# Chunked attention and a multiplicative FFN on one core: a,b of 1024 tokens ahead of the weight product, and w3 turned on the vector engine

## The chip, the cores and the metric

One core of a Trainium2 chip. Times are device microseconds (us) of one execution. The kernel before takes 272.34 us (median of four runs, 271.72 to 272.89), its profiled execution spans 270.6 us.

## The reference, cut to what matters

```python
# q, k, v: (8 batches, 8 heads, 576 positions, 64); attention within chunks of 64
scores = scale * matmul(q_c, k_c.T)
attn   = exp(scores - max) / sum
out    = matmul(attn, v_c)
x = out as (4608 tokens, 512)
a, b = x @ w1, x @ w2                   # 512 -> 1024
return ((a * b) @ w3) @ w_out           # 1024 -> 1024 -> 512
```

Both kernels use (a*b) @ (w3 @ w_out): the weight product `w3o` is formed once on the chip, which needs w3 turned (w3 transposed as the stationary operand).

## The kernel before

A *unit* is 128 tokens (two chunks). Its attention takes four steps, each of them the TensorE part of one *slot*: `t` turns q and k, `s` makes the scores, `p` multiplies exp(scores) by v (with a column of ones for the sum), `x` turns the normalised result into `xt`. Between the steps work the scalar engine (exp) and the vector engine (copies, normalisation). A slot can hold the steps of up to four different units, and the kernel keeps everything on TensorE in program order.

```python
    def do_slot(xu=None, tu=None, su=None, pu=None):
        if tu is not None or su is not None:
            pa = ps.tile([P, 2, 512], f32, tag="pa", name="pa")   # one buffer: turned q,k and scores
        if xu is not None or pu is not None:
            pb = ps.tile([P, 2, 512], f32, tag="pb", name="pb")
        # ... 16 matmuls for xu, 32 for tu, 16 for su, 16 for pu, then
        #     ACT: e = exp(pa);  DVE: qkT = copy(pa), xt = copy(pb), rc = 1/sum, xn = pb * rc
```

The FFN goes by tiles of up to 512 tokens. `do_a`/`do_b` make one of eight 128-row groups of a or b (4 matmuls each), `do_o` makes the output of 128 tokens (8 matmuls). Turning w3 is TensorE work here, eight 128x128 transposes to a row block, and a copy (0.69 us each in the trace) out of PSUM, where the kernel puts the tiles that TensorE writes:

```python
    tiles = [(0, TT), (TT, TT // 2), (TT + TT // 2, TT // 2)]      # TT = 512 tokens
    tiles += [(t0, TT) for t0 in range(2 * TT, NT, TT)]

    def do_w3T(ko):
        tp = ps.tile([P, FO, P], bf, tag="m", bufs=4, name="w3tp")
        for ki in range(FO):
            tr(tp[:, ki, :], w3[:, ko, ki * P:(ki + 1) * P], ident[:])
        w3T_t[ko] = msb.tile([P, FO, P], bf, tag="w3T", bufs=3, name="w3T")
        nc.vector.tensor_copy(w3T_t[ko][:], tp[:])
```

The order at the start: w3 and w_out are loaded first, and the attention of units 0 to 3 is woven into the eight groups of the weight product. Only then follow a,b of tile 0.

```python
    load_w3(0, 1); load_w3(1, 2); load_w(wo, moe_w_out, 0, DM); load_to(1)   # shortened
    load_w3(2, 3); load_w3(3, 4); load_v(0); load_to(3); load_w3(4, 6); load_w3(6, 8)
    # ... w1, w2 in halves, units 4 to 9, v of batch 1
    do_w3T(0); do_w3T(1); do_w3o(0)
    do_slot(tu=0)
    do_w3o(1)
    do_slot(tu=1, su=0)
    # ... 
    do_slot(xu=3)
    do_w3o(7)
    # then a,b of tile 0 (all a, then all b), outputs 0 to 3 with slots between, tiles 1, 2, ...
```

The softmax here doesn't subtract the row's maximum and nothing guards it: scores larger than these inputs give would overflow.

Of the kernel before, what the change touches and what calls it, by code (L numbers as in the profile page):

```python
# [11 lines left out]
def kernel(  # L12
# [53 lines left out]

    ident = consts.tile([P, P], bf, name="ident")
    w1 = wpool.tile([P, KO, DF], bf, name="w1")
    w2 = wpool.tile([P, KO, DF], bf, name="w2")
    w3 = wpool.tile([P, FO, DF], bf, name="w3")  # L70
# [4 lines left out]
    NV = 3  # L75
    vbuf = [consts.tile([P, NHP, NCH, VW], bf, name=f"vbuf{i}") for i in range(NV)]
    for i in range(NV):
        nc.vector.memset(vbuf[i][:, :, :, D:D + 1], 1.0)


    def chunk_at(u, ci):
        return divmod(2 * u + ci, NCH)

    NRAW = 10
    qk_t = {}

    def load_unit(u):

        qk_t[u] = io.tile([P, 2, DM], bf, tag="qk", bufs=NRAW, name="qk")
        (b0, c0), (b1, c1) = chunk_at(u, 0), chunk_at(u, 1)  # L90
        parts = [(0, P, b0, c0)] if b0 == b1 else [(0, CH, b0, c0), (CH, P, b1, c1)]
        for t, src in enumerate((q, k)):
            for p0, p1, b, c in parts:
                load(qk_t[u][p0:p1, t, :].rearrange("p (h d) -> p h d", d=D),
                     src[b, :, c * CH:c * CH + p1 - p0, :].rearrange("h p d -> p h d"))

    def load_v(b):
        for t in range(2):
            load(vbuf[b % NV][t * CH:(t + 1) * CH, :, :, 0:D].rearrange("p n c d -> p (n c) d"),
                 v[b, t * NHP:(t + 1) * NHP].rearrange("n (c p) d -> p (n c) d", p=CH))  # L100
# [5 lines left out]



    NM = NHP // 2
    HW = NHP * CH  # L110
    W = D + 1
    half = [slice(0, CH), slice(CH, P)]
    qkT_t, e_t, xn_t = {}, {}, {}

    def do_slot(xu=None, tu=None, su=None, pu=None):
# [5 lines left out]
        if xu is not None:  # L121
            xn = xn_t.pop(xu)
            xv = pb[:, :, 512 - NHP * CH // 2:512].bitcast(bf).rearrange("p r (n t) -> p r n t", t=CH)
            for n in range(NHP):
                for g in range(2):
                    for r in range(2):
                        tr(xv[half[g], r, n, :], xn[half[r], (2 * n + g) * D:(2 * n + g + 1) * D],
                           ident[half[r], half[r]])
        if tu is not None:
            qk = qk_t.pop(tu)  # L130
            tv = pa[:, :, HW:512].bitcast(bf).rearrange("p r (s n t) -> p r s n t", s=2, t=CH)
            for s in range(2):
                for n in range(NHP):
                    for g in range(2):
                        for r in range(2):
                            tr(tv[half[g], r, s, n, :],
                               qk[half[r], s, (2 * n + g) * D:(2 * n + g + 1) * D],
                               ident[half[r], half[r]])
        if su is not None:
            qkT = qkT_t.pop(su)  # L140
            sv = pa[:, :, 0:HW].rearrange("p r (m c q) -> p r m c q", m=NM, c=2)
            for ci in range(2):
                for m in range(NM):
                    for t in range(2):
                        for r in range(2):
                            mm(sv[half[t], r, m, ci, :], lhsT=qkT[half[r], ci, 1, 2 * t + m, :],
                               rhs=qkT[half[r], ci, 0, 2 * t + m, :], start=True, stop=True)
        if pu is not None:
            e = e_t.pop(pu)
            for m in range(NM):  # L150
                for r in range(2):
                    for ci in range(2):
                        b, c = chunk_at(pu, ci)
                        for t in range(2):
                            n = 2 * m + r
                            mm(pb[half[ci], t, n * W:(n + 1) * W], lhsT=e[half[t], r, m, ci, :],
                               rhs=vbuf[b % NV][half[t], n, c, 0:W], start=True, stop=True)
        if su is not None:
            e = asb.tile([P, 2, NM, 2, CH], bf, tag="e", name="e")
            nc.scalar.activation(e[:].rearrange("p r m c q -> p r (m c q)"), pa[:, :, 0:HW],  # L160
                                 Exp, scale=scale, bias=0.0)
            e_t[su] = e
        if tu is not None:
            qkT_t[tu] = asb.tile([P, 2, 2, NHP, CH], bf, tag="qkT", bufs=3, name="qkT")
            nc.vector.tensor_copy(qkT_t[tu][:].rearrange("p r s n t -> p r (s n t)"),  # L165
                                  tv.rearrange("p r s n t -> p r (s n t)"))
        if xu is not None:
            nc.vector.tensor_copy(  # L168
                xt[:, :, xu * UT:(xu + 1) * UT].rearrange("p n (r t) -> p r n t", r=2), xv)
        if pu is not None:  # L170
            pv = pb[:, :, 0:NHP * W].rearrange("p t (n w) -> p t n w", w=W)
# [4 lines left out]
            xn_t[pu] = xn[:].rearrange("p t n d -> p (t n d)")  # L176


    tiles = [(0, TT), (TT, TT // 2), (TT + TT // 2, TT // 2)]
    tiles += [(t0, TT) for t0 in range(2 * TT, NT, TT)]  # L180
    ab_t, a_t = {}, {}

    def mm_ab(w, dst, t, j):
        t0, n = tiles[t]
        for ki in range(KO):
            mm(dst[:, 0:n], lhsT=w[:, ki, j * P:(j + 1) * P], rhs=xt[:, ki, t0:t0 + n],
               start=(ki == 0), stop=(ki == KO - 1))

    def do_a(t, j):
        n = tiles[t][1]  # L190
        a_ps = ps.tile([P, TT], f32, tag="m", bufs=4, name="a_ps")
        mm_ab(w1, a_ps, t, j)
        a_t[j] = msb.tile([P, TT], f32, tag="a_sb", bufs=FO, name="a_sb")
        nc.scalar.copy(a_t[j][:, 0:n], a_ps[:, 0:n])  # L194

    def do_b(t, j):
        n = tiles[t][1]
        if t not in ab_t:
            ab_t[t] = msb.tile([P, FO, TT], bf, tag="ab", name="ab")
        b_ps = ps.tile([P, TT], f32, tag="m", bufs=4, name="b_ps")  # L200
        mm_ab(w2, b_ps, t, j)
        nc.vector.tensor_mul(ab_t[t][:, j, 0:n], a_t.pop(j)[:, 0:n], b_ps[:, 0:n])  # L202

    def do_ab(t, j):
        do_a(t, j)
        do_b(t, j)

    def do_o(t, n):
# [4 lines left out]
        o_sb = msb.tile([P, DM], f32, tag="o_sb", name="o_sb")  # L213
        nc.scalar.copy(o_sb[:], o_ps[:])  # L214
        r0 = tiles[t][0] + n * P
        inorder(nc.sync.dma_start(out[r0:r0 + P, :], o_sb[:]))
# [3 lines left out]
    def do_w3T(ko):  # L220
        tp = ps.tile([P, FO, P], bf, tag="m", bufs=4, name="w3tp")
        for ki in range(FO):
            tr(tp[:, ki, :], w3[:, ko, ki * P:(ki + 1) * P], ident[:])
        w3T_t[ko] = msb.tile([P, FO, P], bf, tag="w3T", bufs=3, name="w3T")
        nc.vector.tensor_copy(w3T_t[ko][:], tp[:])
# [10 lines left out]
    w3v = moe_w3.rearrange("(ko p) n -> p ko n", p=P)  # L236

    def load_w3(k0, k1):
        load(w3[:, k0:k1, :], w3v[:, k0:k1, :])

    loaded = [0]

    def load_to(u):

        while loaded[0] <= min(u, NU - 1):
            load_unit(loaded[0])
            loaded[0] += 1

    def slot(s):

        do_slot(*(u if 0 <= u < NU else None for u in (s - 3, s, s - 1, s - 2)))

    load_w3(0, 1)
# [4 lines left out]
    load_w3(1, 2)  # L258
    load_w(wo, moe_w_out, 0, DM)
    load_to(1)  # L260
    load_w3(2, 3)
    load_w3(3, 4)
    load_v(0)
    load_to(3)
    load_w3(4, 6)
    load_w3(6, 8)
    HF = DF // 2
    for w, ap in ((w1, moe_w1), (w2, moe_w2)):
        for n0 in range(0, DF, HF):
            load_w(w, ap, n0, n0 + HF)  # L270
    load_to(5)
    load_v(1)
    load_to(9)


    do_w3T(0)
    do_w3T(1)
    do_w3o(0)
    do_slot(tu=0)
    do_w3o(1)  # L280
    do_slot(tu=1, su=0)
    do_w3T(2)
    do_w3T(3)
    do_w3o(2)
    do_w3o(3)
    do_slot(tu=2, su=1, pu=0)
    do_w3T(4)
    do_slot(xu=0, tu=3, su=2, pu=1)
    do_w3T(5)
    do_w3o(4)  # L290
    do_slot(xu=1, su=3, pu=2)
    do_w3T(6)
    do_w3o(5)
    do_slot(xu=2, pu=3)
    do_w3T(7)
    do_w3o(6)
    do_slot(xu=3)
    do_w3o(7)

    load_v(2)  # L300
    load_to(13)


    fill, units = [], {}

    def place(d, f, *a, **kw):
        def run():
            f(*a, **kw)
            if "tu" in kw:
                load_to(kw["tu"] + NRAW)  # L310
        units.setdefault(len(fill) + d, []).append(run)

    def place_slot(d, s):
        place(d, slot, s)
        place(d, load_to, s + NRAW)

        for b in range(B - 3):
            if (NCH * b + NCH - 1) // 2 == s - 2:
                place(d, load_v, b + 3)

    for j in range(FO):
        fill.append(lambda j=j: do_a(0, j))
    place(4, do_slot, tu=4)
    place(6, do_slot, tu=5, su=4)
    for j in range(FO):
        fill.append(lambda j=j: do_b(0, j))
    place(0, do_slot, su=5)
    place(1, do_slot, pu=4)
    place(1, load_v, 3)
# [75 lines left out]
```

## Time and profile before

| | before |
|---|---|
| time, median of 4 | 272.34 us |
| span of the profiled run | 270.6 us |
| TensorE busy | 242.6 us |
| first a,b matmul starts | 42.9 us |
| w3 transposes on TensorE | 64 in 8 groups, 0.55 us a group warm, 1.03 cold |
| weight product | 64 matmuls, 1.73 us a group of eight when warm |
| steady step (slot, two a,b pairs, one output) | 6.06 us |

The chain of waits of the kernel before (the work that ended last, followed back from step to step to what released it), in order of time (start, us, what):

```profile
3.04 10.65 DMA wo<-in_moe_w_out_dram
...
18.61 11.30 DMA w_76<-in_moe_w_dram
...
43.06 4.53 PE a_ps L59 x21
...
76.56 1.60 issue
...
83.06 1.03 issue
...
123.45 1.73 PE o_ps L59 x8
...
129.51 1.73 PE o_ps L59 x8
```

Until 30 us loads set the pace: w_out, then w3. From about 119 us one step follows the other every 6.06 us (129.51 - 123.45) without a gap. "issue" is time in which TensorE waited for nothing that the profile shows.

Two groups of the kernel before, the turning of w3 on TensorE and the copy on the vector engine (busy us, mean ns of one; idle before it):

```profile
L62 PE MATMUL w3tp<-ident,w_76 128*128 128x128 bf16 x64 | 6.4, 265 | 9.5 <-DMA w_76<-in_moe_w_dram 9.5
L225 DVE COPY w3T<-w3tp 128x1024 bf16<-128x1024 bf16 x8 | 5.5, 684 | 11.8 <-PE w3tp L62 11.8
```

Two of its waits (who waited for what: us in total, times, longest):

```profile
PE wp L59 <- DMA wo<-in_moe_w_out_dram: 5.4, 1, 5.4
...
ACT o_sb L214 <- DMA out_dram<-o_sb: 4.7, 2, 3.4
```

### The profile page before, as it was taken

The page shows a single profiled execution, that of the slowest core. Times are in us where ns is not written, and L with a number is a line of the kernel's source. Part 1 is how long each engine was busy: PE and PEld are TensorE (multiplying, and loading weights), DVE is VectorE, ACT ScalarE, POOL GpSimd, SP SyncE. Part 2 cuts the span into 40 slices and gives each one's busy share as a digit, 9 for nine tenths or more (in the row PEclk, how much of TensorE's full clock was granted, in tenths as well). Part 3 has the DMA queues.
Part 4 walks back from the last instruction along what each step waited for, and adds up shares of the span by engine and source line. Part 5 has one row for each costly group of instructions (what it writes and reads, how often), then busy time and mean ns, then how long its engine had stood idle before and what let it go on. Part 6 is the DMA issues. An engine that isn't in the chain of part 4 may idle for free.

```text
span 270.6 us, 8708 instructions
## 1 busy us (share of the span) xinstructions
PE 242.6 (90%) x3896; PEld 127.0 (47%) x3936; DVE 121.4 (45%) x235; ACT 91.2 (34%) x161; POOL 93.9 (35%) x113
## 2 busy tenths in 40 slices
PE   1198599999867999999999999999999999999994
PEld 1135454445655655454444454444444544444441
DVE  1113560364556546775555445555454454332210
ACT  1003125322433343443433344433433343233331
POOL 8484327988857077555422520000000000000000
PEclk9999799999999999999999999999999999999998
DMA  5999999999999999999997991211111111111223
GB/s 87 166 175 169 210 204 158 156 156 202 200 157 142 65 124 155 172 77 151 115 95 84 102 143 45 76 43 41 41 41 41 41 41 70 47 41 39 78 78 118
DMA packets 121620, 29.39 MB, mean 109 GB/s; under 512 B 112880, under 2 KB 115952, under 8 KB 121584
## 3 DMA queue, kind: packets, MB, share of 16 engines
q0 software_dynamic: 116400, 19.41, 94.3%
q1 hardware_dynamic: 5184, 9.44, 9.4%
q8 instruction: 31, 0.51, 0.8%
q14 instruction: 5, 0.04, 0.0%
HBM read 38.80 MB, written 9.44 MB: 178 GB/s over the span
## 4 chain that ended last, share of the span: by engine, by line
PE 78%; DMA 10%; issue 3%; DVE 3%; POOL 2%; ACT 2%; ACTq 0%; POOLq 0%
PE a_ps L59 22%; PE b_ps L59 21%; PE o_ps L59 21%; DMA w_76<-in_moe_w_dram 4%; DMA wo<-in_moe_w_out_dram 4%; PE pa L62 3%; PE pb L62 3%; PE wp L59 3%; DMA out_dram<-o_sb 2%; PE pa L59 2%; PE pb L59 2%; DVE qkT L165 1%; POOL qk L65 1%; DVE xn L175 1%; PE w3tp L62 1%
## 5 line engine op out<-in xcount | busy, mean ns | idle before, releaser
L202 DVE TENSOR_TENSOR ab<-a_sb,b_ps 128x512 bf16<-128x512 f32 (+1 forms) x80 | 50.1, 630 | 57.4 <-PE b_ps L59 52.3
L59 PE MATMUL b_ps<-xt,w_75 128*128 128x512 bf16 (+1 forms) x316 | 74.1, 357 | 0.8 <-ACT o_sb L214 0.3
L59 PE MATMUL a_ps<-xt,w_74 128*128 128x512 bf16 (+1 forms) x294 | 72.3, 357 | 1.6 <-issue 0.5
L59 PE MATMUL o_ps<-w3o,ab 128*128 128x512 bf16 x283 | 66.7, 379 | 0.5 <-issue 0.3
L194 ACT COPY a_sb<-a_ps 128x512 f32<-128x512 f32 (+1 forms) x80 | 43.4, 543 | 49.8 <-PE a_ps L59 47.4
L65 POOL DMA_DIRECT2D qk<-in_q_dram x40 | 34.1, 854 | 46.7 <-PE pa L59 21.9
L59 PEld LDWEIGHTS <-w_75 128*128 128x128 bf16 x320 | 31.1, 98 | 31.4 <-issue 0.8
L214 ACT COPY o_sb<-o_ps 128x512 f32<-128x512 f32 x36 | 21.1, 586 | 66.8 <-PE o_ps L59 62.1
L59 PEld LDWEIGHTS <-ab 128*128 128x128 bf16 x288 | 27.6, 98 | 32.6
L59 PEld LDWEIGHTS <-w_74 128*128 128x128 bf16 x320 | 28.6, 98 | 26.4
L65 POOL DMA_DIRECT2D qk<-in_k_dram x40 | 34.2, 858 | 5.6 <-DMA w_76<-in_moe_w_dram 3.6
L165 DVE COPY qkT<-pa 128x1024 bf16<-128x1024 bf16 x36 | 24.9, 691 | 20.1 <-PE pa L62 13.6
L168 DVE COPY xt<-pb 128x512 bf16<-128x512 bf16 x36 | 15.3, 424 | 40.8 <-PE pb L59 38.1
L160 ACT ACTIVATE e<-pa 128x512 bf16<-128x512 f32 x36 | 21.5, 598 | 28.9 <-PE pa L59 27.1
L175 DVE TENSOR_TENSOR xn<-pb,rc 128x512 bf16<-128x512 f32 x36 | 24.8, 690 | 1.0
L59 PE MATMUL wp<-wo,w3T 128*128 128x512 bf16 x59 | 16.6, 427 | 6.4 <-DMA wo<-in_moe_w_out_dram 5.4
L62 PE MATMUL pa<-ident,qk 64*64 64x64 bf16 x1152 | 16.2, 196 | 1.5 <-issue 1.0
L62 PEld LDWEIGHTS <-qk 64*64 64x64 bf16 x1152 | 12.9, 111 | 6.0 <-issue 5.8
L62 PEld LDWEIGHTS <-xn 64*64 64x64 bf16 x576 | 7.5, 108 | 16.0 <-issue 9.9
L62 PE MATMUL w3tp<-ident,w_76 128*128 128x128 bf16 x64 | 6.4, 265 | 9.5 <-DMA w_76<-in_moe_w_dram 9.5
L233 ACT CAST w3o<-wp 128x512 bf16<-128x512 f32 x8 | 4.7, 586 | 29.9 <-PE wp L59 29.9
L62 PE MATMUL pb<-ident,xn 64*64 64x64 bf16 x576 | 11.6, 199 | 1.9 <-DVE xn L175 1.7
(27 smaller groups left out, 93.6 us busy)
## 6 DMA issues: line engine op xcount, KB each, us to landing
out_dram<-o_sb SPq DMA_DIRECT2D x36, 256.0 KB, 2.9
qk<-in_q_dram POOLq DMA_DIRECT2D x32, 128.0 KB, 6.5
qk<-in_k_dram POOLq DMA_DIRECT2D x32, 128.0 KB, 6.4
vbuf_80<-in_v_dram POOLq DMA_DIRECT2D x6, 288.0 KB, 8.5
vbuf_81<-in_v_dram POOLq DMA_DIRECT2D x6, 288.0 KB, 6.8
vbuf_82<-in_v_dram POOLq DMA_DIRECT2D x4, 288.0 KB, 7.0
w_76<-in_moe_w_dram POOLq DMA_DIRECT2D x4, 256.0 KB, 7.9
wo<-in_moe_w_out_dram POOLq DMA_DIRECT2D x1, 1024.0 KB, 10.6
```

The source lines that it names most:

```text
L59: return inorder(nc.tensor.matmul(*a, **kw))
L62: return inorder(nc.tensor.transpose(*a, **kw))
L65: return inorder(nc.gpsimd.dma_start(dst, src))
L160: nc.scalar.activation(e[:].rearrange("p r m c q -> p r (m c q)"), pa[:, :, 0:HW], Exp, scale=scale, bias=0.0)
L165: nc.vector.tensor_copy(qkT_t[tu][:].rearrange("p r s n t -> p r (s n t)"), tv.rearrange("p r s n t -> p r (s n t)"))
L168: nc.vector.tensor_copy(xt[:, :, xu * UT:(xu + 1) * UT].rearrange("p n (r t) -> p r n t", r=2), xv)
L175: nc.vector.tensor_mul(xn[:], pv[:, :, :, 0:D], rc.to_broadcast([P, 2, NHP, D]))
L194: nc.scalar.copy(a_t[j][:, 0:n], a_ps[:, 0:n])
L202: nc.vector.tensor_mul(ab_t[t][:, j, 0:n], a_t.pop(j)[:, 0:n], b_ps[:, 0:n])
L214: nc.scalar.copy(o_sb[:], o_ps[:])
L233: nc.scalar.copy(w3o[:, ko, :], wp[:])
```

## The change

Its intent: start a,b of the first 1024 tokens as soon as attention of the first units is there, so that the loads of w3 and w_out pass behind that work, and take the turning of w3 off TensorE. The vector transpose is used by blocks of 32x32 (`BL`): w3 is loaded with its column blocks spread over the partitions, and w_out to match. Further: v is loaded by unit and not by batch, the small matmuls inside a slot and their places in PSUM are arranged anew, a and b are made in pairs from the start, three output buffers for two.

```diff
-    w3 = wpool.tile([P, FO, DF], bf, name="w3")
+    w3 = wpool.tile([P, DF // BL, DF // NB], bf, name="w3")          # BL = 32, NB = 4
+    def load_w3(f0, f1):
+        for i in range(NB):
+            load(w3[i * BL:(i + 1) * BL, f0:f1, :],
+                 moe_w3.rearrange("(f y) n -> y f n", y=BL)[:, f0:f1, i * DF // NB:(i + 1) * DF // NB])
+    # load_wo() likewise: four loads of 32 partitions
-    tiles = [(0, TT), (TT, TT // 2), (TT + TT // 2, TT // 2)]
+    tiles = [(0, 4), (4, 1), (5, 3)] + [(u0, 4) for u0 in range(8, NU, 4)]   # in units of 128 tokens
     def do_w3T(ko):
-        tp = ps.tile([P, FO, P], bf, tag="m", bufs=4, name="w3tp")
-        for ki in range(FO):
-            tr(tp[:, ki, :], w3[:, ko, ki * P:(ki + 1) * P], ident[:])
-        nc.vector.tensor_copy(w3T_t[ko][:], tp[:])
+        nc.vector.transpose(w3T_t[ko][:].rearrange("p k (f y) -> p f k y", y=BL),
+                            w3[:, NB * ko:NB * (ko + 1), :].rearrange("p f (k x) -> p f k x", x=BL))
# loads, now: units 0 to 3 (q, k, v), w1 and w2 in quarters, units 4 to 7, w_out, w3, units 8, 9
# order, now:
+    slot(t=0)
+    slot(t=1, s=0)
+    slot(p=0, s=1)
+    slot(x=0, t=2, p=1)
+    ...                                  # nine slots for units 0 to 3
+    for j in range(FO):
+        do_ab(0, j)                      # 512 tokens; slots of units 4, 5 after j = 4, 5, 6
+    slot(x=4, s=5)
+    for j in range(FO):
+        do_ab(1, j)                      # 128 tokens; slots of units 5 to 7 after j = 1, 3, 5, 6
+    slot(p=7)
+    slot(x=7)
+    for j in range(FO):
+        do_ab(2, j)                      # 384 tokens
+    do_w3T(0)
+    for ko in range(FO):
+        if ko + 1 < FO:
+            do_w3T(ko + 1)
+        do_w3o(ko)
+    for u in range(8):
+        do_o(u)
+        if u < 7:
+            step()                       # one slot of units 8 and on after each output
+    # then tiles of 512 as before: slot, two a,b pairs, one output
```

## The prediction

> **What bounds the kernel now.** TensorE. The busy table gives it 242.6 of 270.6 us. From about 119 us to the end it runs without gaps: the chain of waits repeats one slot (0.78 us), two a,b pairs (3.46) and one output group (1.73), 6.06 us in all. So only the time before 119 us is to be won. There the chain shows DMA, not TensorE, until 43 us: nothing until the first w3 row at 4.8, a 5.4 us wait for w_out until 13.7, a 3.3 us wait for w3 until 30. The first a,b matmul starts at 42.9 us, after 64 w3 transposes, 64 product matmuls and four attention units. A second loss, about 6.5 us, lies between 60 and 120 us (windows): outputs waiting for their DMA with two buffers (3.4 us at worst, in the waits), and attention slots waiting about 2 us each for the vector engine.

> **What the change removes.** 64 TensorE transposes of w3: 8 groups at 0.55 us when warm, 1.03 when cold, about 4.5-5 us on the critical engine; 8 PSUM copies of 0.69 us; the wait for 3 MB of w3 and w_out before a,b.

> **What it adds.** Eight vector transposes of 128x1024 bf16. [...] It hides behind tile 2 and the product (1.73 us a group). Also a 128-token tile: at 69 ns a matmul (w3 transposes of that width, chain) its eight pairs take 4.4 us.

> **The new order, from durations of the trace.** Queue issues of q, k, v take about 0.9 us each, so unit 3's k lands near 14 us; its attention chain (about 4.5 us) puts the first a,b at 19-21 us. TensorE is then cold: the product matmuls ran at 446 ns against 216 warm, [...] so about 2 us are lost. Tile 0 ends near 37 us; weight quarters (about 175 GB/s) keep ahead. The 128-token tile interleaves four slots of dependent attention: about 5 us idle, ending near 49. w3's first half should land at 44-48 us, just before the first vector transpose, queued at about 49 ahead of the a*b products. Tile 2 ends near 59, the product near 74. Eight outputs with seven slots: 95. Tile 3 takes 17 us, so the 6 us rhythm starts at 112-113 instead of 119, and the rest is unchanged, 151.5 us.

> **Prediction.** Profile span about 264 us, time 265.5 us, 2.4% faster. Range 260.5-271.5. Chances: faster by over 2% 0.58, within 2% 0.38, slower 0.04.

> **What would show it.** First a,b matmul at 19-21 us; [...] no TensorE wait for w3; product group back to back at about 59-74; o_sb waits gone; steady step still 6.06 us, starting at 112-113.

> **What would make it wrong.** [...] w3 landing after 49 us: the vector engine, then TensorE, would wait. Later attention data, or more idle in the 128-token tile or the output phase, each moves the sum 1-3 us; the 2% line (266.5) is 1 us away.

The sum came to a span of about 264 us and a time of 265.5 us, in which the transposes, taken as hidden, count for nothing. The 2 us for slow matmuls are in it, and the figures beside them give nearly that: eight matmuls at 446 for 216 ns are 1.8 us. In the trace of the kernel before, the product's matmuls follow each other at about 430 ns from 13.73 to 19.49 us (with a slot between), and at about 216 ns in the group that starts at 22.45 us.

## More of the kernel before

The page of the kernel before, busy time by engine, and two rows of its 40 equal slices (6.8 us each; a digit is the busy share in tenths, or, in PEclk, the share of TensorE's full clock that was granted):

```profile
PE 242.6 (90%) x3896; PEld 127.0 (47%) x3936; DVE 121.4 (45%) x235; ACT 91.2 (34%) x161; POOL 93.9 (35%) x113
...
PE   1198599999867999999999999999999999999994
...
PEclk9999799999999999999999999999999999999998
```

TensorE (PE) is the bound, and it is dense from the sixth slice on except for slices 11 to 13.

## The result, and the profile after

| | before | after |
|---|---|---|
| time, median of 4 | 272.34 us | 275.88 us (275.13 to 276.23) |
| ratio of the fast runs | 1 | 1.0122, 95% interval 1.0088 to 1.0155 |
| span of the profiled run | 270.6 us | 274.0 us |
| first a,b matmul starts | 42.9 us | 22.9 us |

A ratio is the mean time of one kernel's fast runs over that of the other's of the same rounds, so it is not quite the ratio of the medians quoted. The changed kernel is 1.2% slower: less than the 2% that the prediction's chances go by, but the interval leaves out 1. I had said 2.4% faster and a range that ended at 271.5.

The page of the changed kernel, the same rows:

```profile
PE 240.6 (88%) x3834; PEld 122.7 (45%) x3872; DVE 127.2 (46%) x244; ACT 91.5 (33%) x161; POOL 114.7 (42%) x146
...
PE   0346987599999749999999999999999999999994
...
PEclk9999999689999988999999999999999999999999
```

TensorE is dense from the fifth slice on and not from the sixth, but there are three thin places: slices 1 to 4, slices 6 to 8 (the 128-token tile) and slices 14 and 15 (the outputs). In the last two places the granted clock falls too.

The chain of waits of the changed kernel:

```profile
22.91 0.59 PE a_ps L59
...
48.61 1.84 issue
...
53.08 1.44 PE a_ps L59 x4
54.52 1.28 PE b_ps L59 x4
55.80 1.24 PE a_ps L59 x4
57.04 0.65 PE b_ps L59 x4
...
65.76 10.74 PE wp L59 x49
...
93.48 0.97 issue
...
98.56 2.63 issue
...
102.31 2.84 PE o_ps L59 x7
...
126.82 1.73 PE o_ps L59 x8
132.88 1.73 PE o_ps L59 x8
```

No load of w3 or w_out is in it, the product is dense, the steady step is 6.06 us as before. What is new are three "issue" gaps, 5.44 us together, and cold matmuls after two of them: four matmuls of 384 columns take 1.24 to 1.44 us, three times over, where later ones take 0.65, and seven of the output group take 2.84 us where the others take 1.67.

The vector transposes in the list of groups take 1240 ns each:

```profile
L225 DVE STREAM_TRANSPOSE w3T<-w 128x1024 bf16<-128x1024 bf16 x8 | 9.9, 1240 | 2.5 <-PE wp L59 1.4 <-DMA qk<-in_q_dram 1.1
```

**What an issue gap is.** Here are the weight loads of TensorE (PEld) between two of the gaps, from the timeline of the changed kernel (start, us, what, count; idle before). There is one to each matmul (the page counts 3872 of them and 3834 matmuls, of which some records can be missing):

```profile
94.44 0.11 PEld L59 LDWEIGHTS <-ab 128*128 128x128 bf16 x2 [1.46 <-issue]
94.98 0.21 PEld L62 LDWEIGHTS <-xn 64*64 64x64 bf16 x16 [0.42 <-issue]
95.10 0.35 PEld L62 LDWEIGHTS <-qk 64*64 64x64 bf16 x32
95.35 0.23 PEld L59 LDWEIGHTS <-qkT 64*64 64x64 bf16 x16
95.49 0.23 PEld L59 LDWEIGHTS <-e 64*64 64x64 bf16 x16
95.76 1.41 PEld L59 LDWEIGHTS <-ab 128*128 128x128 bf16 x8
98.06 0.21 PEld L62 LDWEIGHTS <-xn 64*64 64x64 bf16 x16 [0.89 <-DVE xn L181]
98.18 0.27 PEld L62 LDWEIGHTS <-qk 64*64 64x64 bf16 x22
101.19 0.21 PEld L62 LDWEIGHTS <-qk 64*64 64x64 bf16 x10 [2.74 <-issue]
```

The second gap stands in the middle of 32 like transposes: 16 of them turn q and 16 k, so after 22 both inputs had been there. From gap to gap there are 2+16+32+16+16+8+16+22 = 128 weight loads, and as many matmuls (127 are recorded): 256 instructions. In the kernel before, the gaps at 76.6 and 83.1 us are also 128 weight loads apart by the same count. The thought to be tested is that TensorE's instructions come in blocks of 256 (the expectations call one a page), and that a block comes late when loads of q, k, v are in flight and slots use instructions up fast (a full slot has 160 and takes 0.78 us).

The trace can be asked directly, since it also records a DMA queue named for instructions. From 98 to 101.3 us the DMA view of the changed kernel has one packet on it (packets, MB, share):

```profile
q8 instruction: 1, 0.02, 1.8%
```

The whole run has 30 packets of 16384 bytes on this queue, for 3834 + 3872 = 7706 recorded instructions of TensorE, 257 to a packet, which agrees with the count between the gaps. Narrow windows of the same view date them. The packet before the end of the second gap starts at 98.95 us, when TensorE has already run dry, takes 0.94 us, and TensorE goes on 1.30 us after it has landed. All 34 "issue" gaps of TensorE over 0.5 us in the 16 traces are of this kind: each ends 1.24 to 1.61 us after such a packet has landed, and each stands at 94 to 96 weight loads beyond a multiple of 128. So I take the gaps for waits for instructions. What is left to the experiments is why the packets come late.

```profile
43.21:46.63 3.42, 2.90 (x113) 2.44 (x110) 2.79 (x9) 1.47 (x6) 1.58 (x3) 1.00 1.45 196
46.63:50.04 3.41, 1.02 (x41) 0.78 (x40) 1.57 (x5) 0.91 (x3) 2.18 (x3) 1.00 1.46 197
50.04:53.45 3.41, 1.43 (x35) 0.89 (x35) 2.03 (x5) 0.00 (x0) 2.19 (x3) 0.50 1.47 195
53.45:56.87 3.42, 3.42 (x12) 1.53 (x11) 1.69 (x3) 0.48 (x1) 2.38 (x3) 0.50 2.35 159
56.87:60.28 3.41, 3.41 (x22) 2.06 (x21) 3.23 (x5) 1.43 (x3) 3.14 (x5) 1.00 2.42 156
```

then in the outputs:

```profile
97.82:101.24 3.42, 0.55 (x42) 0.44 (x46) 0.18 (x1) 0.46 (x1) 2.78 (x4) 1.00 1.92 233
101.24:104.65 3.41, 3.08 (x48) 1.64 (x50) 1.92 (x4) 0.60 (x1) 3.18 (x4) 0.50 2.18 159
```

A stretch in which TensorE is busy for 1.02 of 3.41 us is followed by one at half the clock, that one is thin too (1.43 us), and the dense one after it (3.42 us) still runs at half. No idle stretch was longer than 1.84 us in the first case: TensorE was thinly used there and not idle throughout. The trace records no clock before 19.65 us in the kernel before and before 26.15 us in the changed one, so that PEclk reads 9 in the head, although its matmuls run at half the pace there (four in 1.61 us from 24.78 us, four in 0.86 from 26.39). From the first record on the stretches of all 16 traces agree: where a stretch at full clock was followed by half, TensorE had been busy for 1.60 us of it at most (e6, from 100.54 us), and where it was followed by full, for 1.49 us at least (e13, from 99.24 us).

**Where the 10 us between predicted and measured span lie**, stage by stage (ends read from the chain, prediction as in its text with 20 us for "19 to 21"):

| stage | predicted end | measured end | difference in the stage's own length |
|---|---|---|---|
| attention of units 0 to 3, to the first a,b | 20 | 22.9 | +2.9 |
| tile 0 | 37 | 39.9 | 0 |
| 128-token tile | 49 | 53.1 | +1.2 |
| 384-token tile | 59 | 65.5 | +2.4 |
| weight product | 74 | 79.3 | -1.2 |
| eight outputs, seven slots | 95 | 105.1 | +4.8 |
| tile 3, to the steady step | 112.5 | 122.5 | -0.1 |
| rest | 264 | 274.0 | 0 (151.5 both) |

### The profile page after: what moved, and what is told of

It reads as the page before. It is cut to its first block, busy times and chain, and to the rows that moved or that the text cites. A ratio compares the mean times of both kernels' runs of the same rounds, so it can differ in the third digit from the quotient of the medians.

```text
span 274.0 us, 8642 instructions
## 1 busy us (share of the span) xinstructions
PE 240.6 (88%) x3834; PEld 122.7 (45%) x3872; DVE 127.2 (46%) x244; ACT 91.5 (33%) x161; POOL 114.7 (42%) x146
## 3 DMA queue, kind: packets, MB, share of 16 engines
q0 software_dynamic: 122048, 19.41, 95.3%
## 4 chain that ended last, share of the span: by engine, by line
PE 84%; DVE 6%; issue 4%; ACT 2%; DMA 1%; POOL 1%; ACTq 0%; DVEq 0%; POOLq 0%
PE a_ps L59 24%; PE b_ps L59 23%; PE o_ps L59 21%; PE wp L59 5%; PE pa L62 4%; PE pb L62 4%; DVE xn L181 3%; DVE qkT L170 2%; PE pa L59 2%; PE pb L59 2%; DMA qk<-in_k_dram 1%; ACT e L165 1%; POOL qk L65 1%; DVE xt L173 1%; DVE rc L179 0%
## 5 line engine op out<-in xcount | busy, mean ns | idle before, releaser
L59 PEld LDWEIGHTS <-w 128*128 128x128 bf16 x640 | 58.7, 99 | 63.6 <-issue 5.2
L59 PE MATMUL a_ps<-xt,w 128*128 128x512 bf16 (+2 forms) x293 | 75.6, 364 | 3.6 <-DVE xt L173 1.9
L59 PE MATMUL b_ps<-xt,w 128*128 128x512 bf16 (+2 forms) x318 | 76.7, 363 | 1.9 <-issue 1.8
L208 DVE TENSOR_TENSOR ab<-a_sb,b_ps 128x512 bf16<-128x512 f32 (+2 forms) x80 | 50.3, 630 | 58.5 <-PE b_ps L59 56.0
L203 ACT COPY a_sb<-a_ps 128x512 f32<-128x512 f32 (+2 forms) x80 | 43.4, 542 | 72.2 <-PE a_ps L59 66.0
L65 POOL DMA_DIRECT2D qk<-in_q_dram x40 | 34.6, 870 | 34.8 <-PE pa L59 23.7
L59 PEld LDWEIGHTS <-ab 128*128 128x128 bf16 x288 | 27.9, 99 | 34.8 <-issue 3.1
L65 POOL DMA_DIRECT2D vbuf<-in_v_dram x40 | 34.7, 869 | 5.4 <-DMA w<-in_moe_w_dram 3.9
L173 DVE COPY xt<-pb 128x512 bf16<-128x512 bf16 x36 | 15.3, 424 | 46.0 <-PE pb L59 42.5
L62 PE MATMUL pa<-ident,qk 64*64 64x64 bf16 x1152 | 17.1, 199 | 11.6 <-DMA qk<-in_q_dram 6.2
L59 PE MATMUL wp<-wo,w3T 128*128 128x512 bf16 x62 | 13.9, 379 | 0.1
L59 PE MATMUL pa<-qkT 64*64 64x64 bf16 x576 | 11.7, 200 | 2.0 <-DVE qkT L170 2.0
L65 POOL DMA_DIRECT2D w<-in_moe_w_dram x16 | 11.3, 745 | 3.9 <-DMA wo<-in_moe_w_out_dram 2.9
```

The costliest lines, as they stand in the source:

```text
L59: return inorder(nc.tensor.matmul(*a, **kw))
L62: return inorder(nc.tensor.transpose(*a, **kw))
L65: return inorder(nc.gpsimd.dma_start(dst, src))
L173: nc.vector.tensor_copy(xt[:, :, xu * UT:(xu + 1) * UT].rearrange("p (m b) t -> p b m t", b=2), xv.rearrange("p b m c t -> p b m (c t)"))
L203: nc.scalar.copy(a_sb[:, 0:n], a_ps[:, 0:n])
L208: nc.vector.tensor_mul(ab_t[t][:, j, 0:n], a_sb[:, 0:n], b_ps[:, 0:n])
```

## The experiments

Each median is of four runs, on the same chip and in the same rounds as runs of the kernel before (medians 272.2 to 272.7 us). Differences to the changed kernel go from one call to another; the medians of the kernel before differ by 0.5 us between the calls.

### e1: no loads after unit 9

Its output is wrong, which doesn't matter for the time.

```diff
     def load_unit(u):
+        if u >= NRAW:                      # q, k: reuse the old buffer
+            qk_t[u] = qk_keep[u % NRAW]
+            if u >= NVB:                   # v: likewise from unit 12
+                return
```

> The changed kernel without the loads of q and k after unit 9 and of v after unit 11 (later units reuse old buffers: wrong result on purpose). Order and number of TensorE instructions are the same. Theory FETCH (TensorE ran out of instructions at 93.5 and 98.6 us, 0.97 and 2.63 us long, [...] and the second gap cooled it, 1.1 us more): the two gaps vanish, the one at 48.6 us (1.84 us) stays, time 270 to 272 us. Theory CHAIN (the loss is attention slots waiting for vector and scalar engine with too little matmul work between): gaps named issue are a side matter, time 275 to 276 us.

What stays of FETCH is that the gaps come from the loads in flight.

Measured: 272.37 us (270.9 to 273.3), ratio to the kernel before 0.9979. That is 3.5 us less than the changed kernel, and 0.4 us more than the expected 270 to 272. From the first output to the first full tile it took 22.65 us (80.98 to 103.63) against 26.94 (79.14 to 106.08). Both gaps of the outputs are gone and so is the half clock there. The waits of the slots for the vector engine are still there, 0.37 us each, and the gap in the 128-token tile is still there, 1.71 us. The slot that held the second gap, and the longest "issue" left in the outputs:

```profile
99.11 0.32 PE pb L62 x16
99.43 0.26 PE pa L62 x32
99.69 0.18 PE pa L59 x16
...
102.99 0.27 issue
```

FETCH holds for the outputs: the loads stretch the gaps, since TensorE's instructions are the same. The two packets that ended the gaps in the changed kernel have landed here 2.6 and 2.9 us before the first weight load of their block. They took no less time themselves (1.29 and 1.46 us, there 0.95 and 0.94), so what the loads put off is their start. What holds them back before it, no view shows.

### e2 and e5: no loads of w3 and w_out either

Both have the edit of e1 as well. Their outputs are wrong, which doesn't matter for the times.

```diff
 # e2
-    load_wo(); load_w3(...)
+    nc.vector.memset(wo[:], 0.01)
+    nc.vector.memset(w3[:], 0.01)
 # e5
-    load_wo(); load_w3(...)
+    # transposes read w1, w2 in place of w3, the product reads w1 in place of w_out
```

> As the run without late loads, and w3 and w_out are filled on the chip at the start and not loaded either (wrong result on purpose). FETCH: the gap at 48.6 us (1.84 us) vanishes too, and the next tile no longer starts cold (about 2 us): time 266 to 268.5 us, no issue gap of more than 0.5 us. CHAIN: the tile of 128 tokens waits as before for the vector engine, 275 to 276 us. If the gap stays and the tile is still cold, neither loads nor fetch are its cause.

> The run without late loads, and w3 and w_out neither loaded nor filled: the vector transposes read w1 and w2 in their place and the product reads w1 (wrong result on purpose), so that nothing is put in front of the head, which the fills of the earlier quiet run delayed by 8 us. If loads in flight starve TensorE of instructions, no issue gap over 0.6 us is left, and from the first a,b matmul to the end it takes 2.5 us less than without late loads (248.2 us): about 246, time 270 or a little under. The first pairs of the 384-column tile are expected cold all the same (1.24 to 1.44 us for four matmuls, 0.65 warm), as the quiet run showed: the clock is lost by thin work in the 128-token tile and not by the fetch gap.

Measured: 278.77 and 278.72 us, slower by 6 us than e1, and both expectations of the time missed. Both are faults of the experiment. In e2 the two fills took 3.47 and 6.88 us on the vector engine, where I had expected a moment, ahead of the first copy of q and k. In e5 the scheduler put the vector transposes, whose inputs were now there early, into the queue in front of the last `xt` copy of the head, where they waited for w1 and held up the first a,b by 8 us (30.88 us). What can be read is the rest: from the first a,b to the end e5 takes 245.7 us (276.6 - 30.88), e1 248.25 (271.5 - 23.25), the changed kernel 251.1. The expected 246 is met. No issue gap over 0.6 us is left in e5, and the 384-token tile nevertheless begins with 1.44 us for four matmuls:

```profile
58.98 1.44 PE L59 MATMUL a_ps<-xt,w 128*128 128x384 bf16 x4 [0.53 <-DVE xt L176]
```

So the gap of 1.84 us comes from the loads in flight, and the slow matmuls there come without it too; I put them down to the thin 128-token tile.

### e3: w3 turned on TensorE, all else as changed

```diff
-        nc.vector.transpose(w3T_t[ko][:]..., w3[...]...)      # and block loads
+        for ki in range(FO):
+            tr(tp[:, ki, :], w3[:, ko, ki * P:(ki + 1) * P], ident[:])   # and row loads
+        nc.vector.tensor_copy(w3T_t[ko][:], tp[:])
```

> The changed kernel with only the vector transposes undone: w3 and w_out loaded in rows (3 loads instead of 12), w3 turned on TensorE into PSUM and copied, at the same place in the order. If the vector transposes are hidden as predicted, TensorE gets 64 transposes back, 4.4 us at 0.55 us a group: time 280 to 281 us. If the vector transposes or the loads into 32 partitions cost what the change lost, time is 271 to 276 us.

Measured: 281.8 us, 5.9 us above the changed kernel. So the vector transposes are hidden in the new order, and they and their block loads are not what lost the time; they save what the transposes cost TensorE (eight groups of 0.45 us in this run's chain, 3.6 us) and something besides, which I did not take apart: its gap near the end of the outputs was 3.12 us, and half the clock was granted there for 6.83 us and not 3.41. The 64 transposes and their weight loads are also 128 more instructions, as many as half a block.

### e4: slots of units 8 to 14 after every second group

```diff
         do_w3o(ko)
+        if ko % 2:
+            step()
     for u in range(8):
         do_o(u)
-        if u < 7:
+        if u in (1, 3, 5):
             step()
```

> The changed kernel with the seven attention slots of the product and output phase put one after every second group of eight 512-column matmuls (four in the product, three in the outputs) instead of one after each output. Both theories expect a gain: CHAIN 2 us (the waits of 0.4 us in four slots and a little), time about 274; FETCH more, since a page of 256 instructions now lasts 4.2 / (192/256) = 5.6 us instead of 3.6: the gaps at 93 and 98 us and the cold output group go, about 4.7 us beside the 2, time 269 to 271.

Measured: 271.37 us (270.34 to 271.86; ratio to the kernel before 0.9942, 0.9911 to 0.9974), 4.5 us less than the changed kernel, just outside the expected 269 to 271. Product and outputs take 34.84 us (66.53 to 101.37) and not 40.75 (65.33 to 106.08). Of the two gaps one of 0.55 us is left. The seven slots are spread over product and outputs and not over the outputs alone, so that instructions are used up more slowly (a slot and two groups are 192 in 4.24 us, a slot and one group 176 in 2.51), and as I read it the blocks come in time. The order also takes away waits for the vector engine; the run does not separate the two.

### e6: seven slots in the head for nine

```diff
-    slot(p=0, s=1); slot(x=0, t=2, p=1); slot(x=1, s=2); slot(t=3, p=2); slot(s=3); ...
+    slot(t=2, s=1, p=0); slot(x=0, t=3, s=2, p=1); slot(x=1, s=3, p=2); ...
```

> The changed kernel with the first four units' attention in 7 slots, combined as in the kernel before, instead of 9. If the number of slots makes the first a,b matmul late (22.9 us against the 19 to 21 predicted), it moves to 20.5 to 21 us and the time falls by 2 us. If it is the length of the dependent turn of one slot (scalar exp, vector copy, vector normalise: 2 to 3 us), the seven slots only become longer, the first a,b stays at 22 to 23 us and the time at 275 to 276.

Measured: 277.41 us, and the first a,b at 24.8 us, later than with nine: outside both expectations. The number of slots is not what makes the head long. As I read it, a merged slot waits for the latest of its inputs and hands all of them on late: the third slot now waits 1.61 us for q of unit 2. A gap in the supply of instructions, 0.77 us, also falls into this head.

### e7: 256 and 256 tokens for 128 and 384

```diff
-    tiles = [(0, 4), (4, 1), (5, 3)] + ...
+    tiles = [(0, 4), (4, 2), (6, 2)] + ...
     for j in range(FO):
         do_ab(0, j)
-        # t4 after j=4, s4 after 5, (t5, p4) after 6, (x4, s5) at the end
+        # t4 after j=2, (t5, s4) after 4, (s5, p4) after 5, (x4, t6, p5) after 6, (x5, s6, t7) at the end
     for j in range(FO):
         do_ab(1, j)
-        # (t6, p5) after j=1, (x5, s6) after 3, (t7, p6) after 5, (x6, s7) after 6, p7, x7 at the end
+        # (s7, p6) after j=1, (x6, p7) after 3, x7 after 5
```

> The changed kernel with tokens 512 to 1023 in tiles of 256 and 256 instead of 128 and 384, and the slots of units 4 to 7 spread over tile 0 and the first of them. The stretch from the end of tile 0 to the start of the product took 25.4 us (39.9 to 65.3), of which its own matmuls and slots are worth about 16.5. If thin work between dependent slots lost the rest (waits for the vector engine, a fetch gap of 1.84, a cold clock of about 2.5 us), 5 to 7 us come back: time 269 to 271. If the loads of w3 and w_out are what holds the stretch, nothing comes back: the vector transposes and with them the products wait, 275 to 276.

Measured: 270.36 us (270.29 to 271.7), 5.5 us less than the changed kernel and faster than the kernel before (ratio 0.9934, 0.9907 to 0.9961). The product starts at 58.0 us and not at 65.3, with the clock at full from 26.4 us to the end of the profiled run. The loads of w3 held nothing up. The outputs, where nothing was changed, became longer here: four gaps of 1.14, 1.81, 1.82 and 1.24 us, each 128 weight loads from the next.

### e8 and e9: the orders together

e8 is e6, e4 and e7 in one (with the slots of units 4 to 7 shifted to fit), e9 is e4 and e7 with the nine slots of the changed kernel.

> The changed kernel with all three orders: 7-slot head, two tiles of 256, attention slots of units 8 to 14 after every second group of the product and outputs. If the losses are separate they add up: 275.9 - 4.5 - 6 - (0 to 2) = 263 to 266 us, faster than the kernel before by 2.5 to 3.5%. If they are one loss that moves on to the next narrow place, 268 to 271.

> The changed kernel with its own 9-slot head, tiles of 256 and 256, and the spread slots of units 8 to 14. The retiled run alone reached the product at 58.0 us (the changed kernel at 65.3); the spread run alone went from there to the first full tile after the outputs in 34.8 us (the changed kernel in 40.8). If the two gains stand side by side, the full tile starts at 93 to 94 us, the span is 261 to 263 and the time 263 to 265 us, 3% faster than the kernel before. If the gap in instruction supply or the clock finds another place, 266 to 270.

Measured: e8 269.7 us (ratio 0.9901), e9 266.47 us (266.01 to 267.08; ratio 0.9779, 0.9744 to 0.9815). e8 missed the sum and lies in its second range, but not only for the reason given there: its first a,b comes at 24.1 us (e9: 22.75) and its product starts at 63.6 us (e9: 59.1), so the seven-slot head costs as in e6 and the shifted slots more. In e9 the first full tile after the outputs starts at 95.3 us, later than the 93 to 94 expected, after a gap of 2.12 us that is followed by 3.41 us at half clock. The gains of e4 and e7 stand mostly side by side (10.0 us expected as a sum, 9.4 measured), and the gap in supply found another place.

### e10: the vector transposes alone, in the kernel before

```diff
 # kernel before: w3 and w_out laid out for 32x32 blocks, do_w3T on the vector engine
-    load_w3(0, 1) ... load_w(wo, moe_w_out, 0, DM)     # 6 loads of w3, 1 of w_out, 128 partitions
+    load_w3(0, 2) ... load_wo() ...                    # 12 and 4 loads, 32 partitions each
```

> The kernel before with the vector transposes alone (w3 and w_out laid out and loaded for them: 12 and 4 loads into 32 partitions for 6 and 1 into 128), order of everything else as before. TensorE loses 64 transposes, of which four groups (2.2 to 2.8 us) stand after 30 us where TensorE and not the loads sets the pace: 269 to 271 us if the head is otherwise unchanged. If the smaller loads slow the head (nine more issues of 0.65 us, eight loads at most under way), the first a,b comes later than 42.9 us and the gain is gone, 272 to 277.

The two figures of the last sentence are in the trace of the kernel before: its eight issues of w3 take 0.56 to 0.72 us, and never are more than eight loads issued and not yet landed.

Measured: 275.75 us, ratio 1.0122. The first a,b comes at 46.0 us and not at 42.9. The waits of this run:

```profile
PE wp L59 <- DMA wo<-in_moe_w_out_dram: 15.3, 1, 15.3
DVE w3T L223 <- DMA w<-in_moe_w_dram: 8.3, 2, 7.4
...
PE wp L59 <- DVE w3T L223: 7.0, 2, 4.4
```

The 15.3 us are TensorE's whole time from the start, since it has no transposes left to do before the product; w_out itself came 1.5 us later (15.26 us, before 13.73). The product waits for turned blocks (7.0 us, against 0.3 in the kernel before), and the vector engine for w3. Where the loads set the pace, the vector transposes with their loads cost time; in the new order, where w3 is there in time, they gain it (e3). Whether the number of loads or the vector engine's queue has more of it, this run does not tell.

### e11: the kernel before without late loads

Its output is wrong, which doesn't matter for the time.

```diff
 # kernel before, load_unit: from unit 10 on reuse the buffer of unit u % 10; load_v: only batches 0 to 2
```

> The kernel before without the loads of q and k after unit 9 and of v after the third batch entry (wrong result on purpose). If instruction supply under load is a general loss, its two gaps of 1.60 and 1.03 us at 76.6 and 83.1 us vanish too, and the waits of its outputs for their two buffers (4.7 us in the scalar engine's waits) shrink: 267.5 to 270 us. If the gaps are no matter of loads, they stay.

Measured: 267.76 us, ratio 0.9823. Its two gaps are gone too. So the kernel before pays for the loads as well (4.7 us, in which its waits for output buffers are counted too), and of the two kernels without late loads the changed one is still the slower (272.37 against 267.76 us, in different calls): starved instructions made my number wrong, but they do not make the difference between the kernels.

### e12: one more load to a slot

```diff
         slot(...)
+        if s < 16:
+            extra = io.tile([P, DM], f32, tag="extra", bufs=4, name="extra")
+            inorder(nc.sync.dma_start(extra..., q[b, :, c * CH:c * CH + P, :]...))   # read by nobody
```

> The changed kernel with one more load (256 KB, 256-byte pieces, to a tile that nobody reads) per slot of units 8 to 15, issued on the queue of the outputs: right result, the same instructions on TensorE. If loads in flight delay the pages of instructions, the two gaps of the output phase grow from 3.6 us to 5 us or more in sum, and the time to 277.5 to 281 us. If the gaps have another cause, 275 to 277 us.

Measured: 283.55 us (282.72 to 285.35), above the expected range. The chain of this run in the outputs:

```profile
95.18 2.63 issue
...
101.92 3.45 issue
...
110.76 2.73 issue
```

8.8 us for 3.6, again 128 weight loads apart, with more half clock after them. The packet that ended the second of these gaps started at 103.06 us, 1.1 us after TensorE had run dry, and took 0.93 us. With e1 this is a dose and its answer: no loads, no gaps; the loads as they are, 3.6 us; more loads, 8.8 us.

### e13 and e14: the head without the wait for the exponential

In the head the copy of the turned q and k waits for the exponential of the same slot, which shares a PSUM tile with it. Two tiles that are unused then take its place.

```diff
-            tv = pa[:, :, HW:512]...
+            if tu < 4:
+                tm = [ps.tile([P, 2, NHP, CH], bf, tag="m", bufs=4, name="tm") for _ in range(2)]
+            else:
+                tv = pa[:, :, HW:512]...
```

> The changed kernel with the turned q and k of units 0 to 3 in PSUM tiles of their own (two that are free in the head) and two vector copies of 512 elements (about 0.42 us each) for one of 1024 (0.69), so that the copy no longer waits for the exponential of the same slot. If that wait sets the pace of the head, the first a,b matmul moves from 22.9 to 21 to 21.8 us and the time falls 1 to 2 us, to 274 to 275. If the chain exponential, product, normalise, turn, copy does, it stays within 0.6 us of 22.9 and the time at 275 to 276.5.

> The retiled and spread order (266.5 us, first a,b at 22.75) with the same own tiles in the head. 264.5 to 265.5 if the head gains and nothing later gives it back; 266 to 267 if not. The gap in instruction supply at the end of the outputs (2.12 us there) comes at the same instruction and may change in length with the time by which the loads are ahead.

Measured: e13 274.8 us (273.66 to 275.2), first a,b at 21.9 us: this wait was worth 1.0 of the 2.9 us. The time alone would not show it, as the intervals of the ratios of e13 (1.0088) and of the changed kernel (1.0122) overlap; the profile does. e14 264.89 us (263.65 to 266.84; ratio 0.9742, 0.9685 to 0.9798), first a,b at 21.3 us. It is the fastest version found, 2.6% faster than the kernel before, and it computes the right result.

## Why the prediction was wrong, point by point

- **"The wait for 3 MB of w3 and w_out before a,b" goes: right.** No wait of TensorE for w3 or w_out is left; the product is dense, 13.8 us.
- **Of the vector transposes, "It hides behind tile 2 and the product": right.** The transposes took 1.24 us each, a group of the product 1.73, and e3 shows that undoing them costs 5.9 us.
- **"o_sb waits gone" (the waits for output buffers), steady step 6.06 us, the rest 151.5 us: right.** All three are in the chain after.
- **"69 ns a matmul" in the 128-token tile: wrong, in its favour.** Four take 0.22 us, 55 ns each. That hid 0.9 us (64 x 14 ns) of what the tile lost elsewhere, which was luck.
- **"The first a,b at 19-21 us": wrong by 2.9 us, from its middle.** I took the last k's landing and added one unit's chain. The slots of four units wait for each other in program order. e13 gives 1.0 us of it to one shared PSUM tile; e6 shows that fewer slots do not help; the rest is not taken apart.
- **"Eight outputs with seven slots: 95", "Tile 2 ends near 59" and "about 5 us idle, ending near 49": the steps that failed.** The outputs took 25.8 us and not 21, tile 2 12.4 and not 10, the 128-token tile 13.2 and not 12. I counted waits between engines, and slow matmuls only at the first a,b. In their place the runs showed 5.44 us of instruction supply (1.84 + 0.97 + 2.63) and about 3.2 us of half clock (tile of 384: 1.44 + 1.28 + 1.24 - 3 x 0.65 = 2.0; output group: 2.84 - 1.67 = 1.2). With the head that is 11.5 us, with the product's -1.2 it is 10.3 of the 10.0 to be explained. e1, e5, e11 and e12 show the first, the stretches of the clock and e7 the second.

Why the change is slower than the kernel before is a different question. The first a,b starts 20.0 us earlier, but 18.2 us of TensorE work have left that stretch (transposes 8 x 0.55, product 8 x 1.73), so the head lost only about 2 us of idle time. As I read the two orders, that work had filled the waits of dependent slots. In the new order the slots of units 4 to 7 stand among matmuls of 128 columns: 41.1 to 53.1 us for about 3.5 us of a,b (sixteen fours of 0.22) and 2.2 us of slots, 6.3 us lost and then 2.0 to the clock. The slots of units 8 to 14 stand among outputs of 1.73 us. e7 takes back 5.5 us by the tiles alone and e4 4.5 us by the placing of slots alone, and either is enough to beat the kernel before. The 4.4 us of transposes saved could not pay for both. What else was changed (v by unit, the inside of a slot, three output buffers) was not tried alone; the steady step, which has all of it, is 6.06 us in both kernels.

Open: how much of the head is left to gain, why e10 lost as much as it did, and what holds the packets of instructions back while loads are in flight.

## What to carry to other kernels

Moving dense work out of a stage that waits does not gain the wait: look at what the dense work was filling, and put one piece of it, longer than the chain of a dependent step, between each two such steps. Count instructions as well as time: where many tiny matmuls ran while loads were in flight, idle "issue" stood here in the middle of a group (up to 3.45 us, in e12), and 256 instructions on stood the next. And a stage that was merely thin, not idle, cost the dense stage after it its clock here: TensorE was busy for 1.02 of 3.41 us, and the first matmuls of the 384-token tile lost 2.0 us.
